# Casting the w_out weights inside the transfer, and issuing some of the first keys and values from ScalarE

## The chip, the cores and the metric

The kernel runs on one core of a Trainium2 chip. The metric is the device time of one execution in microseconds (us). "Before" and "after" are the two kernels. A profiled execution is timed too; that of the kernel before is not one of the three runs of its median. Its span, from its first to its last recorded event, is about 2 us shorter than its time (186.1 against 187.86 us for the kernel before).

## The reference

Attention over four batches of eight heads of 768 rows and 64 columns, then a small dense network. Three heads see the whole triangle below the diagonal; the other five see a window of 64 rows and four first columns.

```python
scores = scale * np.matmul(q, k.transpose(0, 1, 3, 2))      # B, H, S, D = 4, 8, 768, 64
mask = np.where(retr[0, :, 0, 0, None, None], full_mask, stream_mask)
a = softmax(np.where(mask[None, :, :, :], scores, -1e9))    # written out in the original
x = np.matmul(a, v).transpose(0, 2, 1, 3).reshape(3072, 512)
g = np.maximum(x @ w1, x @ w2)                              # w1, w2: 512 x 1024
return g @ w_out                                            # w_out: 1024 x 512, all float32
```

## The kernel before

A planner inside the kernel orders all operations by estimated costs, and the instructions are then written in that order on each engine. Heads are treated in pairs; a batch has four pairs. What matters here is the loading.

The first three blocks of V of batch 0 (all heads) and one quarter of w_out are issued by ScalarE at the very start; the rest by SyncE. The w_out quarters land as float32 in a staging tile and are cast to bf16 by whichever engine the planner picks:

```python
for n in range(NB // 2):
    nc.scalar.dma_start(out=v_half[:, :, n * D:(n + 1) * D], in_=v[0, :, ...])
for name, c in EARLY:                       # EARLY = (('wo', 3),)
    load_weight(name, c, nc.scalar)
...
wo_ops.append(P.op(lambda e, c=c: copy(e, wo_bf[:, 2 * c:2 * c + 2, :], w_raw[2][:, 2 * c:2 * c + 2, :]),
                   {"DVE": 0.62, "ACT": 0.92}, prio=44 + c, shared=True, **landed(("wo", c))))
```

For each pair, q, k and the rest of V are loaded, one load for each head. In batch 0 a V load is the second half of the rows (96 KB), a q or k load is 192 KB:

```python
for i, src in enumerate((q, k, v)):
    ...
    n0 = NB // 2 if b == 0 and src is v else 0
    for h in range(2):
        two.append(P.op(lambda e, ...: nc.sync.dma_start(out=t.t[:, h, n0:], in_=src[b, ...]), {"SP": 0.55}, ...))
```

Then q and k are cast, transposed by TensorE, and copied out of its accumulators, half by ScalarE and half by VectorE. V is cast by two operations: its first half (already there) by GpSimd or ScalarE, its second half by GpSimd or VectorE:

```python
for p0, p1 in ((0, 64), (64, 128)) if b == 0 else ((0, 128),):
    tk.append(P.op(lambda e, ...: copy(e, tok(qk.t[:, i])[:, p0:p1], ...), {"DVE": ..., "ACT": ...}, [o], [bk, qk], prio=r))
def fv(e):
    for h in range(2):
        copy(e, vb.t[:, h, n0:, 0:D], raws[2].t[:, h, n0:])
ov.append(P.op(fv, {"POOL": 0.58, "DVE": 0.48} if b == 0 else {"POOL": 0.95}, loads[2], ...))
```

In the built program the loads of SyncE and ScalarE share eight completion semaphores in turn, so each such issue waits for the load eight before it. GpSimd's loads have semaphores of their own. This is a fact of the program, not of the chip.

The softmax here doesn't subtract the row's maximum and nothing guards it: scores larger than these inputs give would overflow.

## Time and profile before

| | before |
|---|---|
| median of 3 runs, us | 187.55 (186.88 to 187.66) |
| span of the profiled run, us | 186.1 |
| TensorE busy, us | 170.2 (91%) |
| TensorE's idle time before 35 us | 9.6 |
| TensorE's first matmul behind the wait for the last w2 cast, us | 34.68 |

The last row is called "the door" below, as in the prediction: from there on TensorE hardly idles.

### The profile page before, as it was taken

The numbers are of one execution on the slowest core, as the hardware profiler recorded it, in microseconds if no ns is written. First come the engines' busy times: TensorE is split into PE (matmuls) and PEld (weight loads), VectorE is DVE, ScalarE is ACT, GpSimd is POOL, SyncE is SP. The second block draws the span as 40 slices with busy tenths as digits, with TensorE's granted clock in tenths as the row PEclk, the third lists the DMA queues.
The fourth block names the chain that finished last, engine by engine and source line by source line (L and its number), as shares of the span: only waits on it lengthen the run. The fifth ranks groups of instructions, "written<-read, shape, count | busy, mean of one in ns | idle before, by whom it ended". The sixth has DMA issues, their size and how long they took to land.

```text
span 186.1 us, 4594 instructions
## 1 busy us (share of the span) xinstructions
PE 170.2 (91%) x1643; PEld 100.6 (54%) x1663; DVE 88.0 (47%) x250; ACT 115.8 (62%) x195; POOL 50.7 (27%) x108
## 2 busy tenths in 40 slices
PE   1969988799999999999999999999999999999990
PEld 1845755556755655665565466446555545545460
DVE  5567775768778486544478165354743000000000
ACT  2546998878887678717894386368844624426330
POOL 2101331456796865623025234200000000000000
PEclk9985999999999999999999999999999999999999
DMA  6999999999999899999999999994016612022022
GB/s 142 303 272 356 288 335 354 248 289 311 324 255 249 187 223 221 239 239 176 262 227 240 237 207 202 331 175 174 5 58 188 96 60 113 0 80 89 4 113 70
DMA packets 79553, 36.96 MB, mean 199 GB/s; under 512 B 68642, under 2 KB 73506, under 8 KB 79522
## 3 DMA queue, kind: packets, MB, share of 16 engines
q1 hardware_dynamic: 76130, 35.27, 76.7%
q10 hardware_dynamic: 3392, 1.31, 2.7%
q8 instruction: 15, 0.25, 0.6%
q14 instruction: 16, 0.13, 0.2%
HBM read 25.17 MB, written 6.29 MB: 169 GB/s over the span
## 4 chain that ended last, share of the span: by engine, by line
PE 67%; DMA 15%; issue 4%; SPq 3%; POOL 2%; DVE 2%; DVEq 0%; ACT 0%; POOLq 0%
DMA raw<-in_moe_w_dram 12%; PE mm L786 12%; PE mm L762 10%; PE po L762 7%; PE po L623 7%; PE mm L793 6%; PE sc L578 6%; PE po L786 5%; PE sc L786 4%; DMA ld<-in_q_dram 3%; PE po L793 3%; PE sc L762 2%; PE sc L793 2%; SPq L671 2%; PE mm L695 1%
## 5 line engine op out<-in xcount | busy, mean ns | idle before, releaser
L599 ACT ACTIVATE at_all<-sc 128x1024 bf16<-128x1024 f32 (+2 forms) x72 | 59.8, 869 | 7.3 <-PE sc L578 3.6
L301 POOL CAST qb<-ld 128x384 bf16<-128x384 f32 x51 | 24.5, 508 | 25.1 <-DVE at_all L610 16.9
L762 PEld LDWEIGHTS <-wd_bf 128*128 128x128 bf16 x256 | 23.2, 98 | 14.4 <-POOL wd_bf L443 0.4
L762 PE MATMUL mm<-xt,wd_bf 128*128 128x384 bf16 x136 | 26.8, 326 | 0.2 <-POOL wd_bf L443 0.2
L623 PE MATMUL po<-vb,at_all 128*128 128x65 bf16 x472 | 26.6, 196 | 0.3 <-POOL vb L301 0.2
L623 PEld LDWEIGHTS <-at_all 128*128 128x128 bf16 x472 | 21.9, 99 | 9.0 <-issue 1.4
L578 PE MATMUL sc<-qk 64*128 64x128 bf16 (+2 forms) x364 | 23.1, 240 | 2.2 <-POOL qk L301 0.8
L642 DVE TENSOR_TENSOR xs<-po,rz 128x192 f32 x64 | 22.9, 357 | 2.9 <-DVE rz L639 0.6
L786 PEld LDWEIGHTS <-raw 128*128 128x128 bf16 x152 | 14.2, 98 | 13.8
L578 PEld LDWEIGHTS <-qk 64*128 64x128 bf16 x364 | 12.6, 95 | 14.7 <-issue 10.2
L786 PE MATMUL mm<-wo_bf,raw 128*128 128x512 bf16 (+1 forms) x75 | 18.9, 368 | 0.3
L301 POOL CAST vb<-ld 128x384 bf16<-128x384 f32 (+1 forms) x30 | 13.5, 475 | 20.8 <-DMA ld<-in_v_dram 8.8
L639 DVE RECIPROCAL rz<-po 128x6 f32<-128x6 f32 x32 | 6.2, 193 | 26.0 <-PE po L623 26.0
L762 PE MATMUL po<-xt,wd_bf 128*128 128x384 bf16 x92 | 18.1, 326 | 0.0
L299 ACT COPY ot<-mm 128x512 f32<-128x512 f32 (+1 forms) x12 | 6.8, 567 | 13.2 <-PE mm L793 11.6
L610 DVE TENSOR_TENSOR at_all<-at_all,smk 128x1024 bf16<-128x1024 bf16 (+3 forms) x27 | 14.9, 571 | 0.0
L793 PEld LDWEIGHTS <-xt 128*128 128x128 bf16 x100 | 9.3, 98 | 9.3
L793 PE MATMUL mm<-wm_bf,xt 128*128 128x512 bf16 (+1 forms) x55 | 13.9, 371 | 0.1
L610 DVE TENSOR_TENSOR at_all<-at_all,tri 128x256 bf16<-128x256 bf16 (+1 forms) x36 | 10.1, 313 | 6.6 <-ACT at_all L599 6.5
L695 PEld LDWEIGHTS <-qb 128*128 128x128 bf16 x108 | 7.2, 103 | 5.0 <-DVE qb L301 2.6
L299 ACT COPY vb<-vb 4x256 bf16<-4x256 bf16 (+1 forms) x16 | 6.1, 380 | 6.2 <-PE po L623 6.1
L770 ACT ACTIVATE raw<-mm 128x384 bf16<-128x384 f32 x17 | 8.3, 490 | 2.5 <-PE mm L762 2.2
(91 smaller groups left out, 188.5 us busy)
## 6 DMA issues: line engine op xcount, KB each, us to landing
ld<-in_q_dram SPq DMA_DIRECT2D x32, 192.0 KB, 4.9
ld<-in_k_dram SPq DMA_DIRECT2D x32, 192.0 KB, 4.6
out_dram<-ot SPq DMA_DIRECT2D x23, 256.0 KB, 2.5
ld<-in_v_dram SPq DMA_DIRECT2D x24, 192.0 KB, 4.0
raw<-in_moe_w_dram SPq DMA_DIRECT2D x8, 512.0 KB, 7.5
raw<-in_moe_w_out_dram SPq DMA_DIRECT2D x3, 512.0 KB, 5.8
xt<-in_v_dram ACTq DMA_DIRECT2D x3, 256.0 KB, 3.4
ld<-in_v_dram SPq DMA_DIRECT2D x8, 96.0 KB, 4.3
```

The costliest lines, as they stand in the source:

```text
L299: nc.scalar.copy(out=o, in_=i)
L301: issued[e].append((V if e == "DVE" else nc.gpsimd).tensor_copy(out=o, in_=i).ins)
L578: nc.tensor.matmul(sc.t[:, k, off:off + w], lhsT=qk.t[64 * h:64 * h + 64, 1, j * 128:(j + 1) * 128], rhs=qk.t[64 * h:64 * h + 64, 0, q0:q0 ...
L599: nc.scalar.activation(out=a.t[:, k:k + m, 0:n], in_=sc.t[:, k:k + m, 0:n], func=ACT.Exp, scale=scale, bias=0.0 if bias is None else bias[ ...
L610: issued["DVE"].append(V.tensor_mul(out=y, in0=y, in1=z).ins)
L623: nc.tensor.matmul(po[u].t[:, 0, o:o + D + 1], lhsT=a.t[:, k, off + t * 128:off + (t + 1) * 128], rhs=vb.t[:, h, j, :], **fresh(u))
L642: V.tensor_tensor(out=xs[b].t[:, n0:n0 + nn, bass.ds(col(s0 + h), D)], in0=p4[:, i, :, 0:D], in1=rz_[:, i].unsqueeze(2).to_broadcast([128, ...
L695: nc.tensor.transpose(psb[:, n * 128:(n + 1) * 128], qb.t[:, i, n].rearrange("p h d -> p (h d)"), ident)
L762: nc.tensor.matmul(bk.t[:, 0, 0:GT], lhsT=wd_bf[:, c, f * 128:(f + 1) * 128], rhs=xt[b].t[:, g * NB // NG:(g + 1) * NB // NG, c, :], start ...
L770: nc.scalar.activation(out=gt.t[:, f, :], in_=bk.t[:, 0, 0:GT], func=ACT.Relu)
L786: nc.tensor.matmul(bk.t[:, 0, 0:m1 - m0], lhsT=gt.t[:, f, t * 128:(t + 1) * 128], rhs=wo_bf[:, f, m0:m1], start=(f == 0), stop=False)
L793: nc.tensor.matmul(bk.t[:, 0, 0:m1 - m0], lhsT=xt[b].t[:, c0 // 128, c, :], rhs=wm_bf[:, c, m0:m1], start=False, stop=(c == KC - 1))
```

## The change

The intent: the four casts of w_out are saved by letting GpSimd's queue cast during the transfer, straight into the bf16 tile; and SyncE's row of loads at the start is shortened by issuing six of them from ScalarE. The core of the diff:

```diff
-    w_raw = [raw[:, i, :].rearrange("p (c f) -> p c f", f=f)
-             for i, f in enumerate((d_ff, d_ff, d_model))]
+    w_raw = [raw[:, i, :].rearrange("p (c f) -> p c f", f=d_ff) for i in range(2)]
...
-        dst, arr = {..., "wo": (w_raw[2], moe_w_out)}[name]
+        dst, arr = {..., "wo": (wo_bf, moe_w_out)}[name]
         if name == "wo":
-            rows, cols = slice(c * FC // 4, (c + 1) * FC // 4), slice(0, d_model)
+            rows, cols, queue = slice(c * FC // 4, (c + 1) * FC // 4), slice(0, d_model), nc.gpsimd
...
-            wo_ops.append(P.op(lambda e, c=c: copy(e, wo_bf[:, 2 * c:2 * c + 2, :], w_raw[2][:, 2 * c:2 * c + 2, :]),
-                               {"DVE": 0.62, "ACT": 0.92}, prio=44 + c, shared=True, **landed(("wo", c))))
+            wo_ops.append(P.op(lambda e: None, {"DVE": 0.62, "ACT": 0.92}, prio=44 + c, shared=True, **landed(("wo", c))))
...
+                queue = nc.scalar if b == 0 and (src is v and p < 2 or src is k and p == 0) else nc.sync
                 for h in range(2):
-                    two.append(P.op(lambda e, t=t, src=src, h=h, order=order, n0=n0: nc.sync.dma_start(
+                    two.append(P.op(lambda e, t=t, src=src, h=h, order=order, n0=n0, queue=queue: queue.dma_start(
```

Left out: the w_out load at the start moves behind GpSimd's three iotas, and a guard for the now empty operations.

More of the change, by code (lines that the diff above doesn't have):

```diff
@@ L303, in load_weight @@
     def load_weight(name, c, queue=nc.sync):
-        dst, arr = {"w1": (w_raw[0], moe_w1), "w2": (w_raw[1], moe_w2), "wo": (w_raw[2], moe_w_out)}[name]
+        dst, arr = {"w1": (w_raw[0], moe_w1), "w2": (w_raw[1], moe_w2), "wo": (wo_bf, moe_w_out)}[name]
         if name == "wo":
-            rows, cols = slice(c * FC // 4, (c + 1) * FC // 4), slice(0, d_model)
+            rows, cols, queue = slice(c * FC // 4, (c + 1) * FC // 4), slice(0, d_model), nc.gpsimd
         else:
@@ L322 @@
                                 in_=v[0, :, n * 128:(n + 1) * 128, :].rearrange("h p d -> p h d"))
-        for name, c in EARLY:
-            load_weight(name, c, nc.scalar)
         for o, pattern, cm in ((rel, [[1, 256]], -1), (row, [[1, 1]], 1), (hid, [[1, H]], 0)):
@@ L327 @@
                            allow_small_or_imprecise_dtypes=True)
+        for name, c in EARLY:
+            load_weight(name, c, nc.scalar)
         V.memset(one, 1.0)
@@ L824, in run @@
                 o.emit(o.engine)
-                if o.engine == "DVE" and o.shared:
+                if o.engine == "DVE" and o.shared and issued["DVE"]:
                     held = issued["DVE"][-1]
```

## The prediction

In its part on the Trainium skill, the 0.50 is the granted clock of TensorE, the column in front of the DMA share.

> **What bounds the kernel now.** I began with the page's first part.
>
> ```profile
> PE 170.2 (91%) x1643; PEld 100.6 (54%) x1663; DVE 88.0 (47%) x250; ACT 115.8 (62%) x195; POOL 50.7 (27%) x108
> ```
>
> TensorE is busy for 170.2 of 186.1 us, so 15.9 us of idling is all that a change in loading could win outright. Where it lies is told by the busy time of the engines in five stretches (columns: stretch, its length, then busy us and instructions of PE, PEld, DVE, ACT, POOL, the granted clock, the DMA share, GB/s).
>
> ```profile
> 0.00:10.00 10.00, 4.97 (x48) 4.72 (x48) 5.66 (x30) 3.64 (x7) 1.64 (x12) 1.00 0.82 225
> 10.00:20.00 10.00, 8.33 (x93) 5.32 (x92) 6.51 (x17) 6.37 (x9) 1.15 (x3) 0.66 1.04 316
> 20.00:35.00 15.00, 12.13 (x183) 8.29 (x183) 10.89 (x29) 13.61 (x24) 3.89 (x11) 1.00 0.99 313
> 35.00:60.00 25.00, 24.41 (x299) 15.62 (x299) 18.91 (x48) 20.85 (x32) 18.30 (x29) 1.00 1.01 285
> 60.00:186.00 126.00, 120.39 (x1033) 66.65 (x1045) 46.01 (x129) 71.30 (x126) 25.68 (x56) 1.00 0.72 157
> ```
>
> From 35 us on TensorE idles 0.59 us up to 60, then 5.61, of which about 4.8 are the last output's copy and store after its last matmul at 181.3. So a gain has to be made before 35 us and reach TensorE there as an earlier start of its full stretch. Before 35 the idle time is 5.03 + 1.67 + 2.87 us. The first part holds also 4.66 us of dummy matmuls on the identity, so real work begins at 9.69. Next to it, DMA is full from 10 us on (shares 0.99 to 1.04), and ScalarE is 13.61 of 15 us busy between 20 and 35.
>
> The start, in the order of time (start, length, engine, instruction, in brackets the idle time before it and its releaser):
>
> ```profile
> 8.24 1.04 ACT L299 CAST wo_bf<-raw 128x1024 bf16<-128x1024 f32 x1
> 11.37 0.48 ACT L299 COPY qk<-mm 128x384 bf16<-128x384 bf16 x1 [0.66 <-PE mm L695]
> 11.90 0.39 PE L578 MATMUL sc<-qk 64*128 64x384 bf16 x4 [0.57 <-ACT qk L299]
> 12.76 3.07 ACT L599 ACTIVATE at_all<-sc 128x1024 bf16<-128x1024 f32 x3 [0.92 <-PE sc L586]
> 13.76 0.69 DVE L301 CAST wo_bf<-raw 128x1024 bf16<-128x1024 f32 x1 [1.32 <-DMA raw<-in_moe_w_out_dram]
> 17.16 1.02 ACT L599 ACTIVATE at_all<-sc 128x1024 bf16<-128x1024 f32 x1 [1.32 <-PE sc L586]
> 18.59 1.43 ACT L599 ACTIVATE at_all<-sc 128x1024 bf16<-128x1024 f32 x2 [0.41 <-PE sc L578]
> 19.92 1.04 ACT L299 CAST wo_bf<-raw 128x1024 bf16<-128x1024 f32 x1
> 20.86 1.03 ACT L599 ACTIVATE at_all<-sc 128x1024 bf16<-128x1024 f32 x1
> ```
>
> The reader is to see three things: the transposed keys and queries are copied out by ScalarE and VectorE half each, and the first scores wait for ScalarE's half at 11.37; of the two w_out casts on ScalarE one lies in idle time (8.24), the other between exponentials (19.92); and the gaps at 17.16 and 18.59 wait for TensorE, not for data.
>
> The last view is the chain of waits, with TensorE's longest wait of that time:
>
> ```profile
> 23.03 8.34 DMA raw<-in_moe_w_dram
> 31.39 7.52 DMA raw<-in_moe_w_dram
> ...
> 34.68 0.40 PE L452 MATMUL mm<-ident,w_bf 128*128 128x128 bf16 x4 [0.93 <-DVE w_bf L301]
> ```
>
> At 34.68, the door of the full stretch, TensorE waits 0.93 us for the cast of the last quarter of w2 (on VectorE at 33.93), which waits for its load. So the door opens when the DMA engines have carried everything up to that quarter.
>
> **What the Trainium skill says.** "DMA: Bandwidth & Descriptors", section "Issuing engines are not separate DMA queues": transfers of all issuing engines run on the same 16 DMA engines and interleave; only issue time is saved. The trace agrees as far as it shows: the load is 316 GB/s at 10 to 20 us with SyncE issuing nearly alone, with a DMA share already at 1.04. The same page, "SWDGE vs HWDGE vs iDMA": a cast during the transfer is for GpSimd's queue only, whose software writes the descriptors. No transfer of that kind is in this trace. "SBUF — State Buffer", section "SBUF: two separate sides": while VectorE runs a two-port operation, such as a float32 copy, GpSimd can't write descriptors. The trace can't show it yet, but VectorE casts for 2.70 of 3.40 us between 9.2 and 12.6. "TensorE: Matmul & The Clock Gate", Part 1: the clock halves after a window of about 3.4 us with little work and comes back after a busy one. The trace agrees: 0.50 from about 12.7 to 19.1 us,
>
> ```profile
> 12.60:16.00 3.40, 2.93 (x27) 1.78 (x26) 1.75 (x5) 3.01 (x3) 0.00 (x0) 0.50 1.07 327
> 16.00:19.20 3.20, 3.20 (x39) 2.20 (x37) 2.44 (x6) 1.63 (x2) 1.15 (x3) 0.50 1.07 362
> ```
>
> **The change, part by part.** The plan that orders the work is unchanged (the empty operations keep their planned durations), and the built program shows TensorE's order identical; only the issues and the four casts move.
>
> Casts removed: two of 1.04 us on ScalarE (2.08) and two of 0.69 on VectorE (1.38). On the path: the one at 19.92 delays the next exponential from about 20.0 to 20.86, so 0.9 us; the one at 8.24 and the VectorE ones stand beside waits for loads, so about 0. Sum: 0.9 us of ScalarE's chain.
>
> Issues moved: SyncE loses six loads and the w_out issues. Keys were issued at 6.06, after the queries at 4.85. ScalarE's first stage loses the w_out issue (0.87 us), so its table load and exponential end at about 4.3 instead of 5.21; with the 1.2 us that SyncE spends between the flag and its first load (3.65 to 4.85), ScalarE can issue keys at about 5.5, so 0.6 us earlier. But bytes and engines are the same: in front of the last key (landed at 6.5 + 3.7, about 10.3) lie 786 KB of V, 524 of w_out and 786 of q and k. Keys and queries now share, queries land later by about as much as keys land earlier, and w_out, now in a third ring, slides in beside V. Estimate: the last of the four lands at 10.0 to 10.5, as before. Win about 0.
>
> A new wait on ScalarE: the program uses eight completion semaphores in turn for the hardware queues, and each issue waits for the one eight before it. SyncE met that before. Now ScalarE does, in its own order of work: its issue of the second half of V of the first pair waits for a key load of the first pair; its two V loads of the second pair, which stand between its two copies of transposed q and k, wait for the second pair's first query and first key loads. Those landed before at 14.3 and 15.3 (9 and 10 plus 5.3). With SyncE free sooner it issues them at about 6 and 8 instead of 8.94 and 10.0; up to this key lie 786 + 524 + 786 + 98 + 393 + 197 KB = 2.78 MB plus what two more w_out quarters take by then, say 0.4 MB. At 300 GB/s from 2.2 us that is 12.8 us, so with issue and copy (0.4 + 0.48) the first scores start at about 13.4 instead of 11.9: 1.5 us later. In return the second pair's data are there, so the 0.44 us that TensorE waits for them at 15.22 goes, and part of the delayed work meets the full clock after 19.1. Left at 21 us: 0.5 us late on TensorE, 0.9 early by ScalarE's cast: about level.
>
> DMA: the w_out bytes read are the same 2.1 MB; all of them still stand before the last w2 quarter. So the door at 34.68 moves only by what the lull of DMA (175 to 226 GB/s in some us at 10 and 23) is filled: estimate 0 to 0.7 us. Sum: 187.55 - 0.5 = 187.0.
>
> **Rivals.** First, ScalarE's blocked order costs more than I count: a load landing at 15.3 as before would put the first exponential at about 16.3, 3.5 us late. ScalarE's gaps after it (1.32 + 0.41) and the cast (0.9) give back 2.6, and TensorE's 0.93 us at the door covers the remaining 0.9, so it would end near 188, and 189 if TensorE at half clock is the slower one. Against it: SyncE runs ahead now. Second, the casting transfers are slow, by starved descriptors or half speed in the engines: half speed for 2.1 MB at 300 GB/s is 7 us of DMA in a stretch that DMA fills, the door would move by several us, 191 or more. Nothing in this trace shows such a transfer. Third, the relief counts fully: eight loads ahead without w_out in the line let w2 land earlier, and ScalarE is 0.9 us ahead; with the 0.93 us of the door and the waits of 0.82 at 28.81 and 0.3 each at 24.5 and 26.1, up to 2.4 us, so about 185. Against it: the w2 loads are behind the same bytes.
>
> **Range and chances.** Small gains against small losses, each within 2 us, and a 0.93 us buffer at the door: 187.0, with 185.3 (most of the third) to 189.0 (the first). More than 2% faster needs under 183.8, 3.75 us of the 9.6 idle before 35: 0.06. More than 2% slower needs over 191.3, the second rival: 0.07. Within 2%: 0.87.
>
> **What would show it.** Right: no w_out casts; ScalarE's second copy of q and k behind its loads, the first exponential at 13.5 to 15 us; pair two's exponentials near 20.9; the last w2 cast still at 33 to 34.7; TensorE full from there. Wrong: the first exponential before 12.8 (no blocking), or the last w2 cast more than 1.5 us off (the DMA account), or idling of TensorE after 35 us.

## More of the kernel before

The prediction prints the rows for the stages, the exponentials and the door. Two more groups of lines are needed later, from the timeline of the kernel before: what SyncE issues, and what VectorE does between the casts of the first pair's queries and keys and the first scores. The columns are start, length, engine, line, operation, destination and source, and the number of instructions.

```profile
7.24 0.97 SPq L671 DMA_DIRECT2D ld<-in_v_dram  x2
8.26 0.48 SPq L310 DMA_DIRECT2D raw<-in_moe_w_out_dram  x1
...
11.22 0.60 DVE L301 CAST vb<-ld 128x192 bf16<-128x192 f32 x2
11.88 0.56 DVE L301 COPY qk<-mm 128x384 bf16<-128x384 bf16 x1
```

The two V loads of the first pair are put in ahead of SyncE's first w_out quarter. VectorE casts both halves of them at 11.22 without having waited, and goes straight on to its half of the key copy at 11.88. Note the order on VectorE: the V cast stands in front of the key copy, although TensorE needs the key copy first.

## The result

| | before | after |
|---|---|---|
| median, us | 187.61 (186.88 to 187.73, 4 runs) | 193.19 (191.81 to 193.59, 4 runs) |
| profiled run: time, span, us | 187.86, 186.1 | 191.81, 189.9 |
| door, us | 34.68 | 38.86 |

The ratio of after to before is 1.0293, with a 95% interval of 1.0233 to 1.0353: slower. Ratios are the mean time of one kernel's runs over that of the other's of the same rounds, so they are not quite the ratio of the medians. Executions over 1.5% slower than the fastest of the same kernel are left out of the means. The profiled run of after is the fastest of its four, so its span shows somewhat less than the median loss.

The busy time of the engines in two of the prediction's stretches, now of the kernel after (the same columns: PE, PEld, DVE, ACT, POOL, granted clock, DMA share, GB/s):

```profile
10.00:20.00 10.00, 3.45 (x32) 1.83 (x34) 3.37 (x11) 2.59 (x5) 0.00 (x0) 0.63 1.04 247
20.00:35.00 15.00, 13.24 (x184) 8.94 (x186) 9.28 (x25) 12.59 (x21) 5.10 (x13) 0.91 1.00 293
```

The loss is in the first row: between 10 and 20 us TensorE is busy for 3.45 us where it was 8.33, and all other engines are idler too, while the DMA share is full as before. GpSimd runs no instruction at all. That the DMA engines moved only 247 GB/s instead of 316 is in part a matter of counting: the page counts a casting quarter of w_out as the 256 KB that it writes, a plain one as 512 KB. The same columns in two shorter stretches, the first of which the prediction shows of before:

```profile
16.00:19.20 3.20, 0.16 (x4) 0.13 (x4) 1.03 (x4) 0.00 (x0) 0.00 (x0) 0.50 1.00 262
19.20:23.00 3.80, 3.80 (x39) 2.53 (x36) 1.88 (x6) 2.34 (x3) 1.74 (x4) 0.53 0.92 248
```

In the first of these rows TensorE works 0.16 of 3.20 us. In the second it is busy throughout, but at a mean clock of 0.53, where the kernel before had 1.00. This is not a second loss beside the gap. Between 12.6 and 23 us TensorE was busy at the low clock for about 5.4 us here; the kernel before, whose clock was at 0.50 to about 19.2, was busy at it for 6.1 us. The slow work was moved to a later time, not added to.

Selected lines of the timeline of the kernel after tell who waits for what (in brackets the idle time before an instruction and its releaser), in order of time:

```profile
9.51 0.39 ACTq L670 DMA_DIRECT2D ld<-in_v_dram  x1
10.02 0.60 ACT L298 CAST vb<-xt 128x192 bf16 x2 [1.81 <-DMA ld<-in_k_dram]
13.24 0.61 PE L576 MATMUL sc<-qk 64*128 64x384 bf16 x4 [2.06 <-ACT qk L298]
14.42 1.02 ACT L597 ACTIVATE at_all<-sc 128x1024 bf16<-128x1024 f32 x1 [1.24 <-PE sc L584]
18.16 0.35 DVE L300 CAST vb<-ld 128x192 bf16<-128x192 f32 x1 [5.95 <-DMA ld<-in_v_dram]
18.43 0.55 DVE L300 COPY qk<-mm 128x384 bf16<-128x384 bf16 x1
19.04 0.40 PE L576 MATMUL sc<-qk 64*128 64x128 bf16 x4 [4.33 <-DVE qk L300]
20.01 1.94 ACT L597 ACTIVATE at_all<-sc 128x1024 bf16<-128x1024 f32 x2 [4.56 <-PE sc L584]
```

ScalarE issues the V load of the first pair's second head at 9.51 only. In its order of work this issue stands behind other things, and it has to wait for a key load of the first pair, because it takes that load's completion semaphore; ScalarE's cast right behind shows the wait (1.81 us, released by the load of keys). The load takes 8.6 us from issue to landing. VectorE, in order, waits 5.95 us for it with its half of the key copy standing behind. TensorE waits 4.33 us for that copy, and ScalarE 4.56 us for TensorE. In the kernel before the same load had been issued at about 7.8, the second of the two in the line at 7.24, and took 3.6 us.

The door, from the same timeline (a line of the kernel before is in the prediction), with VectorE's work in front of it:

```profile
35.69 0.20 DVE L637 RECIPROCAL rz<-po 128x6 f32<-128x6 f32 x1 [2.32 <-PE po L621]
...
38.11 0.69 DVE L300 CAST w_bf<-raw 128x1024 bf16<-128x1024 f32 x1
...
38.86 0.40 PE L450 MATMUL mm<-ident,w_bf 128*128 128x128 bf16 x4 [0.43 <-DVE w_bf L300]
```

The last w2 cast, at 38.11, has no bracket: it no longer waits for its load. It stands in VectorE's order behind a normalization of attention results at 35.69, which waited 2.32 us for TensorE. So the door is set by the late attention work, no longer by the bytes.

### The profile page after: what moved, and what is told of

Read it like the earlier page. It is cut to its first block, busy times and chain, and to the rows that moved or that the text cites. A ratio compares the mean times of both kernels' runs of the same rounds, so it can differ in the third digit from the quotient of the medians.

```text
span 189.9 us, 4593 instructions
## 1 busy us (share of the span) xinstructions
PE 169.5 (89%) x1643; PEld 100.3 (53%) x1663; DVE 86.1 (45%) x248; ACT 113.8 (60%) x193; POOL 53.1 (28%) x112
## 4 chain that ended last, share of the span: by engine, by line
PE 79%; ACT 3%; DVE 2%; issue 1%; POOL 0%; DVEq 0%
PE mm L785 12%; PE mm L761 12%; PE sc L576 8%; PE po L621 8%; PE po L761 8%; PE mm L792 6%; PE po L785 5%; PE sc L785 4%; PE po L792 3%; PE mm L461 3%; PE sc L761 2%; PE sc L792 2%; ACT at_all L597 2%; PE mm L694 1%; PE sc L584 1%
## 5 line engine op out<-in xcount | busy, mean ns | idle before, releaser
L761 PEld LDWEIGHTS <-wd_bf 128*128 128x128 bf16 x256 | 23.2, 98 | 13.8
L621 PE MATMUL po<-vb,at_all 128*128 128x65 bf16 x472 | 25.9, 195 | 0.2
L621 PEld LDWEIGHTS <-at_all 128*128 128x128 bf16 x472 | 21.3, 98 | 8.7 <-issue 1.0
L785 PEld LDWEIGHTS <-raw 128*128 128x128 bf16 x152 | 14.1, 98 | 13.8
L300 POOL CAST vb<-ld 128x384 bf16<-128x384 f32 (+1 forms) x30 | 13.4, 475 | 24.3 <-DVE qb L300 10.4
L608 DVE TENSOR_TENSOR at_all<-at_all,tri 128x256 bf16<-128x256 bf16 (+1 forms) x36 | 9.5, 297 | 6.7 <-ACT at_all L597 6.6
```

The lines of the kernel that those rows point to most:

```text
L300: issued[e].append((V if e == "DVE" else nc.gpsimd).tensor_copy(out=o, in_=i).ins)
L608: issued["DVE"].append(V.tensor_mul(out=y, in0=y, in1=z).ins)
L621: nc.tensor.matmul(po[u].t[:, 0, o:o + D + 1], lhsT=a.t[:, k, off + t * 128:off + (t + 1) * 128], rhs=vb.t[:, h, j, :], **fresh(u))
L761: nc.tensor.matmul(bk.t[:, 0, 0:GT], lhsT=wd_bf[:, c, f * 128:(f + 1) * 128], rhs=xt[b].t[:, g * NB // NG:(g + 1) * NB // NG, c, :], start ...
L785: nc.tensor.matmul(bk.t[:, 0, 0:m1 - m0], lhsT=gt.t[:, f, t * 128:(t + 1) * 128], rhs=wo_bf[:, f, m0:m1], start=(f == 0), stop=False)
```

## The experiments

The expectations number the theories. T1: V's small packets, in ScalarE's own queue, go slowly beside the large ones of the others. T2: the casting transfers of GpSimd hold up the rest. T3: ScalarE's own waits, between its copies of transposed queries and keys, make the loss. T4 was formed after the first four runs: V of the first pair is put in late and lands behind what was put in before, whatever its queue and packets, and this late V, by way of VectorE's order, is the loss. The first four ran on one chip, the next four on another, the last two on a third; the kernel before had medians of 187.49, 187.71 and 187.28 us there, and each ratio is against the kernel before on the same chip. "Loss" below means only that the interval lies above 1.

| run | median, us | ratio (95%) | door | span | span - door |
|---|---|---|---|---|---|
| before (profile) | 187.55 | | 34.68 | 186.1 | 151.4 |
| after | 193.19 | 1.0293 (1.0233 to 1.0353) | 38.86 | 189.9 | 151.0 |
| e1_v_wide_packets | 191.36 | 1.0201 (1.0139 to 1.0263) | 38.31 | 189.3 | 151.0 |
| e2_issues_only | 190.62 | 1.0160 (1.009 to 1.023) | 38.14 | 189.0 | 150.9 |
| e3_wo_only | 188.62 | 1.0059 (1.000 to 1.0119) | 36.00 | 187.1 | 151.1 |
| e4_v_pair0_sync | 189.37 | 1.0132 (1.0041 to 1.0223) | 35.99 | 187.0 | 151.0 |
| e5_front | 187.28 | 1.0011 (0.9952 to 1.007) | 33.90 | 185.0 | 151.1 |
| e6_late_v_alone | 191.66 | 1.0211 (1.0174 to 1.0248) | 39.53 | 190.3 | 150.8 |
| e7_wo_late | 189.14 | 1.0067 (1.0022 to 1.0112) | 36.86 | 188.1 | 151.2 |
| e8_wo_all_late | 191.18 | 1.0159 (1.009 to 1.0227) | 38.71 | 189.7 | 151.0 |
| e9_front_v0 | 187.34 | 0.9969 (0.992 to 1.0018) | 35.36 | 186.4 | 151.0 |
| e10_v_pair1_sync | 191.71 | 1.0232 (1.0177 to 1.0288) | 38.05 | 189.4 | 151.3 |

The last column is the first finding. In all twelve profiles what follows the door takes 150.8 to 151.4 us, with the w_out casts or without. So a version's time is decided by when its door opens, as the prediction assumed.

**e1_v_wide_packets.** The V loads of the first two pairs read the rows in another order, so that each packet is 768 bytes, three times as long. Its output is wrong, which doesn't matter for the time.

```diff
                 order, rate = ("(p n)", WIDE) if wide[r] and src is not v else ("(n p)", NARROW)
+                if b == 0 and p < 2 and src is v:
+                    order = "(p n)"
```

> The changed kernel, but the ScalarE-issued halves of V of batch 0 are read in rows of 768 B instead of 256 B (a wrong order of tokens, so a wrong result on purpose): the same bytes, queue, moment and waits, a third of the packets. Theory T1 (the DMA engines take turns between the queues packet by packet, so V's 256 B packets on ScalarE's queue get little beside packets of 1.5 and 2 KB on the other two): the half of V issued near 9.5 us lands in under 5.5 us instead of 8.6, VectorE's wait of 5.95 us for it falls below 2, time 187 to 189. Theory T2 (the casting w_out transfers take the DMA time): same bytes, so V still lands in about 8 us, 191.5 to 193.5. Theory T3 (ScalarE's own waits between its copies make the loss): 191.5 to 193.5.

Measured: 191.36 us. The load was issued at 10.31 (after: 9.51) and took 7.0 us instead of 8.6; VectorE waited 4.59 us for it, TensorE 3.45. So T1's forecast (landing in under 5.5 us, a wait below 2 us, 187 to 189 us) failed, and packets are not the main cause. They may be a part: the wait is shorter by a quarter, and the ratio is 1.0201 instead of 1.0293, though the intervals overlap. The time lies just under the 191.5 that T2 and T3 gave as their least.

**e2_issues_only.** The kernel before with only the six issues moved to ScalarE; w_out is loaded and cast as before.

```diff
+                queue = nc.scalar if b == 0 and (src is v and p < 2 or src is k and p == 0) else nc.sync
-                    ... nc.sync.dma_start(
+                    ... queue.dma_start(
```

> The kernel before with only the six issues moved to ScalarE; w_out stays float32 on SyncE's queue, with its casts. T1: V's small packets meet one queue of large packets instead of two, so they land in 5 to 7 us, time 188.5 to 191. T2: no casting transfer, so 187 to 188. T3: 191 to 193.

Measured: 190.62 us, 3.1 us over the kernel before's 187.49, without any casting transfer. So T2 (187 to 188 us) is no necessary part of the loss. The time lies in T1's range and just under T3's 191. The way of the loss is a different one here, as TensorE's and ScalarE's rows of the timeline show:

```profile
15.75 0.48 ACT L299 COPY qk<-mm 128x384 bf16<-128x384 bf16 x1 [1.83 <-DMA ld<-in_v_dram]
16.29 0.61 PE L578 MATMUL sc<-qk 64*128 64x384 bf16 x4 [2.25 <-ACT qk L299]
```

On ScalarE's queue the keys now stand behind the w_out quarter that ScalarE issues at the start, and SyncE, which has less to do, issues the next w_out quarter at 5.98 instead of 8.26. The keys took 6.2 to 6.7 us, so TensorE waits 3.73 us for the casts and starts the transposes at 12.58. Then ScalarE's two V issues of the second pair, standing between its two copies, block the second copy until 15.75: what T3 describes, in a run in which VectorE waits for V for only 0.26 and 0.97 us.

**e3_wo_only.** The changed kernel with all loads back on SyncE: only the casting transfers are left of the change.

```diff
-                queue = nc.scalar if b == 0 and (src is v and p < 2 or src is k and p == 0) else nc.sync
+                queue = nc.sync
```

> The changed kernel with all six loads back on SyncE: only w_out is bf16 by GpSimd. T1: no small packets on a queue of their own after 8 us, 186.5 to 188. T2: the loss stays, 191 to 193. T3: 186.5 to 188.

Measured: 188.62 us, ratio 1.0059, with an interval from 1.000: a small loss if any, less than T2 asked for (191 to 193) and just above the 188 of T1 and T3. ScalarE's first exponentials start at 12.70 (before: 12.76), so the first pair is untouched. But GpSimd issues two w_out quarters from 8.60 on, among the second pair's loads, where the kernel before issued one (at 8.26; the next at 12.05), and that pair's casts come up to 1.5 us later (the last at 17.39; before at 15.94).

**e4_v_pair0_sync.** The changed kernel with the V loads of the first pair back on SyncE.

```diff
-                queue = nc.scalar if b == 0 and (src is v and p < 2 or src is k and p == 0) else nc.sync
+                queue = nc.scalar if b == 0 and (src is v and p == 1 or src is k and p == 0) else nc.sync
```

> The changed kernel with only V of the first pair back on SyncE; keys of the first pair and V of the second stay on ScalarE. T1: VectorE's wait for V of the first pair goes from 5.95 us to under 2; V of the second pair still lands late, which GpSimd's cast waits for; 187 to 189.5. T2: 192 to 193.5. T3: ScalarE's two waits for the second pair's loads remain, the first exponential stays near 14.4 us, 191 to 193.

Measured: 189.37 us, in T1's range and outside those of T2 and T3. VectorE's wait for V is gone and the exponentials, once begun at 14.58, run on without a gap of more than 0.70 us. The interval is wide (1.0041 to 1.0223), and its profile has the full clock throughout, which no other profile has, so it isn't compared more finely. About half of the loss or more goes with the V loads of the first pair; the run doesn't say whether it is their queue or their time.

**e5_front.** That is what the next two tell apart. In the changed kernel only ScalarE's order is altered: the other three V loads are put directly behind the first. Queues, packets, casting transfers and the engine that issues all stay.

```diff
-        order.sort(key=lambda o: o.start)
+        order.sort(key=lambda o: (o.start, 0) if o.at is None else (o.at if isinstance(o.at, float) else o.at.start, 1))
...
+                if b == 0 and src is v and exact:
+                    if p == 0:
+                        first[0] = two[0]
+                    if p < 2:
+                        for o in two:
+                            if o is not first[0]:
+                                o.at = first[0]
```

> The changed kernel with the second half of V of the first pair and both of V of the second put at the front of ScalarE's order, right behind the first half: they wait only for loads of the start. Same queues, same bytes, same casting transfers, same packets. Theory T4 (a place in line: a load lands when all that any queue issued before it has landed; V's second half was held back on ScalarE until 9.5 us, when SyncE and GpSimd had put about 2.1 MB in front of it): V's second half is issued by 7 us and lands by 12, VectorE's wait of 5.95 us falls below 1.5, second exponential at 14 to 17 instead of 20, time 187.5 to 190. Theory T1 (small packets starve on a queue of their own): V still lands after 15, 191 to 193. Theory T2 (casting transfers): 191 to 193.

Measured: 187.28 us, ratio 1.0011: the loss is gone, as T4 said (the time is just under its range) and T1 and T2 did not. Its timeline:

```profile
12.88 0.61 DVE L301 CAST vb<-ld 128x192 bf16<-128x192 f32 x2
...
14.04 3.07 ACT L599 ACTIVATE at_all<-sc 128x1024 bf16<-128x1024 f32 x3 [1.24 <-PE sc L586]
...
20.86 1.02 ACT L599 ACTIVATE at_all<-sc 128x1024 bf16<-128x1024 f32 x1 [0.65 <-PE sc L586]
...
33.90 0.40 PE L451 MATMUL mm<-ident,w_bf 128*128 128x128 bf16 x4 [0.43 <-DVE w_bf L301]
```

VectorE casts both V halves without a wait. The first exponential is still 1.3 us later than before (14.04 against 12.76), but the one that stood at 20.86 stands at 20.86 again: the gaps and the w_out cast that the kernel before had in between take up the delay. This is what the prediction had expected of the change itself.

**e6_late_v_alone.** The reverse: the kernel before, all loads on SyncE and the casts on the engines, with only SyncE's order altered, so that a w_out quarter and a query load of the third pair go ahead of the second V load of the first pair.

```diff
+                    if exact and (name, c) == ("wo", 1):
+                        d_w[name, c].at = 5.9
...
+                if b == 0 and exact and p == 0 and src is v:
+                    two[1].at = 5.97
+                if b == 0 and exact and p == 2 and src is q:
+                    two[0].at = 5.95
```

> The kernel before, w_out and its casts as they were, everything on SyncE as it was; only SyncE's order is altered, so that V's second half of the first pair comes behind the second pair's queries and keys, a w_out quarter and a query of the third pair. T4: issued near 11.5 us with about 2 MB in front of it, it lands near 18; VectorE waits 5 to 6.5 us for it, and the time is 190.5 to 193.5 without any load on ScalarE or GpSimd. T1 and T2: V stays in SyncE's queue and nothing is cast in transfer, so at most 189.

Measured: 191.66 us, ratio 1.0211, in T4's range and above the 189 of T1 and T2. The load was issued at 11.46; VectorE's wait is a little longer than the 6.5 us forecast. The timeline has the picture of the changed kernel:

```profile
18.20 0.36 DVE L302 CAST vb<-ld 128x192 bf16<-128x192 f32 x1 [6.81 <-DMA ld<-in_v_dram]
...
19.08 0.39 PE L582 MATMUL sc<-qk 64*128 64x128 bf16 x4 [5.58 <-DVE qk L302]
```

A late V load of 96 KB, without any casting transfer and without ScalarE, makes a loss of the same kind and some seven tenths of the size. ScalarE's next exponentials start at 20.05, in the changed kernel at 20.01.

**e7_wo_late** and **e8_wo_all_late** asked for a version that beats both kernels: e3 with two w_out quarters held back on GpSimd until behind the first pairs (issued from 14.83 on), and e8 with the quarter of the start held back as well.

```diff
+                    if exact and (name, c) in (("wo", 1), ("wo", 2)):
+                        d_w[name, c].at = {1: 13.6, 2: 11.5}[c]
```

e8 in addition:

```diff
-        for name, c in EARLY:
-            load_weight(name, c, nc.scalar)
```

with that quarter issued together with `("wo", 2)`.

> Run e3 (only w_out bf16 by GpSimd) with two of its quarters issued behind GpSimd's casts of the second and third pair, near 17 and 19 us instead of 8.3 and 9. T4: queries and keys of the second pair land 1.5 us earlier than in e3 (last key cast on VectorE at 16 instead of 17.4), and e3's loss of 1.1 us goes: 186.5 to 188.2. T2 (casting costs DMA time wherever it stands): as e3, 188 to 189.5.

> As e7, and the w_out quarter of the very start also moved behind GpSimd's first casts. T4: 524 KB less in front of the first queries and keys, so they land about 1.5 us earlier (first cast of queries near 7 us), first exponential at 11 to 11.7; the last quarter of w2 still has the same bytes in front of it, so the door is where it was: 185.5 to 187.5. T2: as e3, 188 to 189.5.

Measured: 189.14 us (ratio 1.0067) and 191.18 us (1.0159). T4's forecasts missed in both; e7's time lies in T2's range, e8's above it. No version that beats both kernels came of this. The first two pairs do come earlier (in e7 the fourth exponential of ScalarE's row at 16.31, before at 17.16), but the bytes held back then lie in front of the third and fourth pair. The longest waits of TensorE between 20 and 33 us, the first line from e7:

```profile
25.63 0.49 PE L698 MATMUL po<-ident,qb 128*128 128x128 bf16 x6 [1.68 <-DVE qb L301]
```

and this one from e8:

```profile
30.88 0.61 PE L578 MATMUL sc<-qk 64*128 64x128 bf16 x8 [3.46 <-POOL qk L301]
```

DMA is full in this stretch (a share of 1.09 in e7 and 1.12 in e8, from 20 to 33 us), so bytes that are moved back seem only to move the wait. T2's reading, that casting costs DMA time wherever it stands, is not refuted by e7 itself; e5 speaks against it, with all four casting transfers and no loss, and so does the trace (see the rivals below).

**e9_front_v0.** The changed kernel with only the first pair's V on ScalarE, both loads in front; the second pair's V back on SyncE. In e5 ScalarE issued V loads until 10.7 and could begin its own cast of V only at 10.89; this version should spare it that.

```diff
-                queue = nc.scalar if b == 0 and (src is v and p < 2 or src is k and p == 0) else nc.sync
+                queue = nc.scalar if b == 0 and p == 0 and src is not q else nc.sync
...
+                    if p == 0:
+                        two[1].at = first[0]
```

> The changed kernel, with the V loads of the second pair back on SyncE and the second half of V of the first pair put at the front of ScalarE's order, right behind the first half; keys stay on ScalarE, w_out stays with GpSimd. If order alone matters (T4), V lands in time, VectorE's wait for it is gone, and since ScalarE no longer stops for the key loads in front of its V casts, its first exponentials are no later than with all V loads in front (14.04): expected 13.0 to 14.0, door 33.0 to 34.5, 186.0 to 188.0 us, ratio 0.99 to 1.005. If ScalarE's stops in front of its V casts were what kept that version from beating the kernel before, this one is the faster of the two by 0.5 us or more, ratio under 0.998.

Measured: 187.34 us, six runs from 186.30 to 190.31 (the last one slow and left out of the ratio), ratio 0.9969 with an interval of 0.992 to 1.0018. VectorE no longer waits for V:

```profile
12.57 0.60 DVE L301 CAST vb<-ld 128x192 bf16<-128x192 f32 x2
...
13.94 3.07 ACT L599 ACTIVATE at_all<-sc 128x1024 bf16<-128x1024 f32 x3 [1.24 <-PE sc L586]
```

ScalarE's cast moves to 7.94 and the first exponential to 13.94, as expected; the expected door of at most 34.5 was missed (35.36), in a profiled run that took 188.52 us, over the median. There VectorE waits 1.69 us for a key load at 25.75, long after the first pair. Whether it is faster than the kernel before by a few tenths is open: the interval contains 1.

**e10_v_pair1_sync.** The changed kernel with only the second pair's V back on SyncE; the first pair's V stays late on ScalarE.

```diff
-                queue = nc.scalar if b == 0 and (src is v and p < 2 or src is k and p == 0) else nc.sync
+                queue = nc.scalar if b == 0 and (src is v and p == 0 or src is k and p == 0) else nc.sync
```

> The changed kernel with only the V loads of the second pair back on SyncE; the second half of V of the first pair stays late on ScalarE. T4 (the late V of the first pair is the loss): VectorE still waits 4 us or more for it, door 38 to 39.5, 190.0 to 193.5 us, ratio 1.015 to 1.03. Rival (the loss comes from ScalarE's V issues of the second pair between its copies of q and k): most of it is gone, 187 to 189 us, ratio under 1.008.

Measured: 191.71 us, ratio 1.0232, as T4 said and the rival did not. VectorE and TensorE still wait:

```profile
17.33 0.36 DVE L300 CAST vb<-ld 128x192 bf16<-128x192 f32 x1 [4.32 <-DMA ld<-in_v_dram]
...
18.20 0.40 PE L576 MATMUL sc<-qk 64*128 64x128 bf16 x4 [3.73 <-DVE qk L300]
```

So the V loads of the second pair, which the prediction had worried about most, carry about the difference of 1.0293 and 1.0232, whose intervals overlap. The cleanest comparison is that of e9 and e10, measured on one chip against the same runs of the kernel before: their kernels differ only in the place of one 96 KB load, V of the first pair's second head, in ScalarE's order. Put in front the ratio is 0.9969, left late it is 1.0232, and the intervals are far apart. So the late V of the first pair carries most of the loss; how much the second pair's issues add is not resolved (e4, which keeps them late, has an interval from 0.4 to 2.2%).

## Why the prediction was wrong

**The door sets the end: right.** Span less door is 150.8 to 151.4 us in every profile, and TensorE doesn't idle much behind it.

**The casts removed: right in busy time, without effect.** VectorE's busy time fell from 88.0 to 86.1 us and ScalarE's from 115.8 to 113.8, near the 1.38 and 2.08 worked out. The 0.9 us that this was to give ScalarE at 20 us could not show: ScalarE was idle there for 4.56 us, waiting for TensorE. It was misread as well. In the kernel before, the last matmul recorded for the scores of the exponential at 20.86 ends at 20.49, so the cast held that exponential up by 0.4 us at most; in e5, without the cast, it starts at 20.86 too, after 0.65 us of waiting for TensorE.

**The keys, 10.0 to 10.5: about right.** VectorE's last three casts of queries and keys run from 9.72 to 10.62.

**The first scores at 13.4: right** (13.24; the terms as written, 12.8 + 0.4 + 0.48, add up to 13.7), and the first exponential at 14.42 lies in the range of 13.5 to 15.

**"Left at 21 us: 0.5 us late on TensorE, 0.9 early by ScalarE's cast: about level": this step failed.** The prediction named the wait of the very load that matters: "its issue of the second half of V of the first pair waits for a key load of the first pair". It then priced only what such waits do to ScalarE's own next work. It didn't ask when that load lands, nor who stands waiting for it: VectorE, in order, with its half of the key copy behind. An estimate, with the issue times of the run: when it was issued at 9.51, what had been put in and not landed was about 98 KB of the first V load, 786 of the second pair's queries and keys, 1,048 of two w_out quarters and 197 of a query load of the third pair, 2.1 MB in all, counted as float32 read; at the 300 GB/s that the prediction used this is 7 us, against 8.6 measured. The line is not strict: a query load of 192 KB that SyncE issued just behind it, at about 9.7, took 7.3 us and so landed ahead of it. VectorE's order, V cast before key copy, is in the timeline of the kernel before. The runs put this in the step's place: a wait of 5.95 us on VectorE, passed on as 4.33 us on TensorE (e9 and e10, which differ by the place of this load alone, stand at 0.9969 and 1.0232; e5 takes the wait away and the loss with it, though it brings the second pair's V forward too; e6 makes such a wait alone and loses 2.1%).

The two first-pair exponentials that stood behind it started at 20.01, where the kernel before ran the second of its three at about 13.8 (12.76 and one of 1.02 us): 6.2 us late. The door came 4.2 us late. So some 2 us were given back on the way. The gaps of 1.32 and 0.41 us and the cast of 1.04 us on ScalarE that the prediction lists are the likely place, but no run took them apart.

**"The door moves by 0 to 0.7 us": failed, and so did the reason.** It moved by 4.2 us, and not by the DMA account: the w2 loads were issued from 21.66 on, where the kernel before began at 21.48, and the last w2 cast didn't wait for its load at all. The prediction had listed a last cast over 1.5 us off as a sign that the account of bytes was wrong. That test was drawn too narrowly, since VectorE's order can delay the cast as well. The account of bytes in front of w2 wasn't tested by this run.

**The rivals.** The first had the right kind, blocked order on ScalarE, but stopped at ScalarE and ended at 188 to 189. The second, slow casting transfers, had the right size (191 or more) for a wrong reason: the door was late, but e2 loses 1.6% without them, and e3, with them alone, is at 1.0059. The page of the kernel after speaks against its "half speed", in the row of GpSimd's queue (packets, MB written, share of the 16 engines' span):

```profile
q0 software_dynamic: 1088, 1.05, 3.5%
```

Of 189.9 us this is 6.6 us of all DMA engines for the 2.1 MB read, about 315 GB/s, which is not slower than the 300 GB/s of the prediction's estimate. The third is the nearest to what e5 and e9 reach, and even they are no faster than the kernel before by more than the intervals allow.

**A slip in a reading.** The 2.70 us of VectorE's casts that the prediction gives between 9.2 and 12.6 us are VectorE's whole busy time; the casts are about 1.7 us of it. Nothing rests on it.

## What to carry to other kernels

Where all DMA engines are full, as here, price an issue by its place in the line first, and not only by its own bytes or by the time that it costs the issuing engine: work out what is in front of it when it goes in, and then look for the engine that waits for it in order, with more urgent work standing behind. Moving issues to another engine changes the place of every load, of those that weren't moved too, because they now go in earlier or later and meet other waits. Check the order in which each engine issues, not only the engine; here a mere reordering made and unmade 2 to 3%.

## What the Trainium skill lacked or had wrong

- "DMA: Bandwidth & Descriptors", section "Issuing engines are not separate DMA queues": it says that transfers of all issuing engines interleave on the same 16 DMA engines and that spreading the issues saves only issue time. The runs agree that nothing is gained, but it lacks that the place in the line is at stake: the same 96 KB load took 3.6 us when issued at 7.8 and 8.6 us at 9.51, and order alone took the ratio from 1.0293 to 1.0011 (e5) and, for this one load, from 1.0232 to 0.9969 (e10 and e9).
- The same page, section "Queues, rings and completion order": each DMA engine takes turns between the queues it has work for, packet by packet. From that one might expect a small load in a queue of its own to overtake a backlog in others. Here it didn't: V, with only the last key load and the first V load before it in ScalarE's queue, took 8.6 us, and 7.0 us with packets three times as long (e1). The page's packet holds several descriptors, so it need not be the 256-byte piece that the profile counts as a packet. The runs don't show why V was so slow.
- The same page, section "SWDGE vs HWDGE vs iDMA": a cast during the transfer is possible on GpSimd's queue only; it gives no time for one. Here a casting transfer of 512 KB read took GpSimd 0.71 to 0.85 us to issue and 5.4 to 8.6 us to land amid the others, where a plain one of the kernel before took a median of 5.8 us between 5 and 20 us. The four took 3.5% of the DMA engines' span, 6.6 us for 2.1 MB read.
- "SBUF — State Buffer", section "SBUF: two separate sides": a two-port operation of VectorE keeps GpSimd from writing descriptors. With VectorE casting float32 beside it, the longest issue in the kernel after was 0.85 us and the median 0.73, and in the other runs with casting transfers none is longer than 0.86; none looks starved.
- "TensorE: Matmul & The Clock Gate", Part 1: it has the clock halved after an idle window of about 3.4 us, and doesn't say how much work still counts as idle. In the kernel before, the clock fell to 0.50 at about 12.4 us although TensorE had been busy for 1.36 us between 8.8 and 12.2, without an idle gap longer than 0.84 us.
